# Infini-attention with a parallel silu layer on one core: odd heads' masked score halves, a memory update by pairs of heads, and a new order of the work

## The chip, the cores and the metric

The kernel runs on one core of a Trainium2 chip. The metric is the device time of one execution, in microseconds (us). The kernel before took 229.18 us in the median of three timed runs (228.67 to 229.85). The engines are called by the profile's names: PE is TensorE (PEld its weight loads), ACT ScalarE, DVE VectorE, POOL GpSimd, SP the engine that issues most DMAs.

## The reference, cut to what matters

```python
xn = layernorm(x)                                   # x: 2048 x 512, bf16
# A: 32 heads of 16 dimensions, 4 segments of 512 positions, M and z start at zero
for s in range(4):
    p = softmax(q @ k.T / 4 + causal_mask)          # within the segment
    a_dot = p @ v
    a_mem = (phi(q) @ M) / (phi(q) @ z + 1e-6)      # phi(t) = t + 1 if t > 0 else exp(t)
    o = sigmoid(beta) * a_mem + (1 - sigmoid(beta)) * a_dot
    M = M + phi(k).T @ v;  z = z + phi(k).sum()
A = o @ wo
# B: silu(xn @ w1) @ w2, with w1 512 x 1792
out = x + A + B
```

## The kernel before

**Layout.** Everything that a product contracts lies transposed: 128 features on the partitions, 512 positions of a segment along the row. A tile of 128 features (`dt`, four of them) holds eight heads of 16, so each block of 32 partitions (a group `g`, four of them) holds an even head in its lower and an odd head in its upper 16 rows.

**Scores.** `scores` (L653) makes one *batch*: PE fills a tile `psS` of four PSUM banks (one bank of 512 columns for each `g`), ACT takes the exponential of all 128 x 2048 in one instruction (L669) into a bf16 buffer `Pb`, and POOL zeroes what the causal mask forbids (`affine_select`, L677). The four matmuls of a chunk (one for each `g`) use 32 rows of the array each and run side by side. Keys are taken in blocks of 128 (`kt`), and for a key block only the queries from its first position on are scored: 512, 384, 256 and 128 columns. That is 1280 columns for each parity of head, 2560 for a `dt`, five batches of 512: 80 batches for 4 segments and 4 `dt`. An even head's keys are read from 16 rows of `kT`; an odd head's from all 32 rows of `kTo`, a copy that POOL makes of `kT` with the even rows set to zero (`k_copy`, L359). There is a single `psS`, so the next batch's matmuls wait for the exponential of the last; seven `Pb` buffers hold the weights.

**Weighing.** `weigh` (L687) multiplies the weights by the values: word `E` for the even heads of a `dt`, `O` for the odd ones, each four chunks of 512, 384, 256 and 128 columns, with 32 columns of the array for each `g` (L696). The values carry a block of ones, which gives the softmax's sums. Copies to SBUF and small DMAs bring the sums together (`zraw`), DVE takes reciprocals, DMAs spread them over the rows (`spr<-rz`), and DVE multiplies.

**Memory.** `m_mm` (L415) multiplies phi(k), transposed by DMA, by the values: for each `dt` and each 128 positions one product of 128 x 128, of which `m_mask` (L437) keeps the eight 16 x 16 blocks on the diagonal.

**The other work.** `dense` gives q, k, v and the hidden layer, `out_mm` (L593) the two output products. `product` (L319) issues such a product as one matmul of 128 columns of the array, or, in a stretch that began with a word of kind "cols", as four matmuls of 32 columns that run side by side.

**The order.** The kernel is written under a manual schedule. `ORDER` (L16) is a list of words, each a call of a small function (`S17` the score batch 17, `k0.2.1` a part of the k product of segment 0 and `dt` 2, `kv` its copy on DVE, `ka` on ACT, `h` hidden, `ha` its tanh, `o`, `oc`, `od` output products whole, halved and quartered, `st` an output's store). Each engine runs its instructions in the order of the list, and waits only on semaphores. The list was made by a planner outside the file. Batches carry numbers `20 s + 5 dt + b`; the first is `S1`. The last output tile is stored in two halves (`half_store`, L628) from buffers of their own, `o_half`.

Of the kernel before, what the change touches and what calls it, by code (L numbers as in the profile page):

```python
# [9 lines left out]
ALU = mybir.AluOpType  # L10
BF16 = mybir.dt.bfloat16
# [5 lines left out]
kind odd ones0 ones1 zeros xc0 xd0 xc1 xq0 xi0 Nv0 busy44 xd1 xq1 xc2 xi1 X0.1 Nv1 xd2 Xa0.1 busy6 v0.0.0 v0.0.1 xq2 X1.1 Xa1.1 xs3 v0.0.2 v0.0.3 xq3 v0.1.0 xi2 v0.1.1 v0.1.2 v0.1.3 Nv2 xi3 X2.1 va0.0 k0.2.0 va0.1 Nv3 Xv2.1 X3.1 Xv3.1 k0.0.0 k0.0.1 k0.0.2 k0.0.3 q0.0.0 kv0.0 tb q0.0.1 q0.0.2 xs4 q0.0.3 qa0.0 k0.2.1 q0.3.0 fa0.0 q0.1.0  # L17
S1 k0.2.2 xs6 q0.1.1 v0.3.0 v0.3.1 xs7 q0.3.1 q0.1.2 q0.1.3 xs5 xg4.4 q0.3.2 qa0.1 q0.3.3 fp0.0
S2 k0.2.3 v0.3.2 qv0.3 v0.3.3 k0.1.0 kv0.2 fp0.2 fa0.2 k0.1.1 vv0.3 k0.1.2 k0.1.3 q0.2.0 q0.2.1
S3 kv0.1 q0.2.2 h0.10.0 h0.10.1 Nv4 fv0.0 q0.2.3 h0.10.2 v0.2.0 h0.10.3 qv0.2 ha0.10 k0.3.0 k0.3.1  # L20
S0 Nv5 v0.2.1 k0.3.2 hv0.10 h0.11.0 k0.3.3 h0.11.1 h0.11.2 kv0.3 h0.11.3 Nv7 xs8 XD5 ha0.11 h0.7.0
S7 h0.7.1 h0.1.0 h0.7.2 h0.7.3 v0.2.2 h0.1.1 v0.2.3 XD4 h0.1.2 h0.1.3 hv0.11 Nv6 ha0.7
S6 h0.13.0 fp0.3 XD7 h0.13.1 vv0.2 hv0.7 E0 XD6 v1.1.0 h0.13.2 h0.13.3 ha0.1 v1.1.1 Ev0
S5 fv0.2 h0.5.0 v1.1.2 h0.5.1 hv0.1 v1.1.3 vv1.1 v1.3.0 h0.5.2 ha0.13 xs14 hv0.13 h0.5.3 ha0.5 t0.2 v1.3.1
S9 hv0.5 xs12 q1.1.0 v1.3.2 v1.3.3 fa0.3 q1.1.1 q1.1.2 E1 k1.1.0 q1.1.3
S4 qv1.1 k1.1.1 vv1.3 fv0.3 k1.0.0 k1.0.1 k1.0.2 lw0 h0.4.0 k1.1.2 Ev1 h0.4.1 k1.0.3 k1.1.3 kv1.1
S17 h0.8.0 h0.8.1 kv1.0 h0.4.2 O0 xs10 h0.4.3 h0.2.0 Ov0 ha0.4
S10 h0.2.1 k1.2.0 xs11 xs9 k1.2.1 h0.2.2 k1.2.2 h0.2.3 h0.8.2 ha0.2 t0.3 hv0.4 xg8.4 t0.0 k1.2.3
S8 hv0.2 q1.0.0 q1.0.1 q1.0.2 kv1.2 q1.0.3 h0.8.3 q1.2.0 ha0.8 q1.2.1 q1.2.2 h0.6.0 fp0.1
S13 q1.2.3 h0.6.1 qv1.0 xs15 O1 h0.6.2 qv1.2 Ov1 v1.2.0 Nv11 fa0.1 hv0.8 h0.6.3 Nv9  # L30
S12 h1.11.0 h1.11.1 v1.2.1 fv0.1 h1.11.2 k1.3.0 h1.11.3 k1.3.1 ha0.6 k1.3.2 k1.3.3 Nv10 fp1.1
S11 kv1.3 XD11 v1.2.2 t0.1 v1.2.3 m0.2 ha1.11 hv0.6 q1.3.0 mv0.2 vv1.2 q1.3.1 h0.3.0
S14 fa1.1 h0.0.0 XD9 q1.3.2 q1.3.3 Nv8 h0.3.1 h0.3.2 hv1.11 E2
S15 h0.0.1 h0.0.2 gp1.0 qv1.3 v1.0.0 Ev2 v1.0.1 v1.0.2 xs13 h0.0.3 ha0.0 xg12.4 v1.0.3 fv1.1 h1.9.0 vv1.0 XD8 hv0.0
S16 h1.9.1 h0.3.3 m0.0 h0.9.0 ha0.3 mv0.0 h1.9.2 h1.9.3 ha1.9 XD10 xl0.0 O2
S19 h0.9.1 Ov2 hv1.9 h0.9.2 E3 h0.9.3 h0.12.0 h0.12.1 Nv12 h0.12.2 Ev3 ha0.9
S18 hv0.3 bmask k2.2.0 h1.0.0 h0.12.3 ha0.12 k2.2.1 h1.0.1 h1.0.2 h1.0.3
S22 kv2.2 v2.1.0 hv0.9 hv0.12 ha1.0 tanh O3 h1.8.0 v2.1.1 h1.8.1
S21 h1.8.2 Ov3 v2.2.0 hv1.0 vv2.1 v2.2.1 o0.0.0 o0.0.8 h1.8.3 vv2.2 od0.0.11.1 ha1.8 o0.0.3 Nv14
S23 h1.10.0 hv1.8 o0.0.2 gate sv0 r0.0 xl0.2 oc0.0.13.1 r0.3 o0.0.10 oc0.0.13.0 o0.0.12 k2.1.0 r0.2 h1.4.0 XD14 lw1 o0.0.6  # L40
S20 k2.1.1 kv2.1 h1.4.1 h1.4.2 h1.4.3 r0.1 w0 z0.3 ha1.4 o0.0.5 h1.10.1 h1.10.2 h1.10.3
S24 ha1.10 k2.0.0 k2.0.1 od0.0.11.2 hv1.4 oc0.0.4.0 o0.0.9 kv2.0 E4 od0.0.11.3 od0.0.11.0
S26 fp1.2 o0.2.4 z0.0 o0.2.1 Ev4 fa1.2 o0.2.7 oc0.2.9.0 hv1.10 q2.3.0 zv0.3 o0.2.13 q2.3.1 qv2.3 oc0.2.2.0
S25 h1.5.0 Nv13 h1.5.1 h1.5.2 z0.2 z0.1 o0.0.7 O4 oc0.2.2.1 Ov4 ga1.0 zv0.0 od0.2.0.1
S27 gv1.0 q2.1.0 oc0.2.9.1 o0.0.1 h1.5.3 fv1.2 ha1.5 o0.2.6 q2.1.1 gp1.1 qv2.1 o0.2.17
S29 o0.2.14 o0.2.3 oc0.0.4.1 o0.1.2 zv0.1 zv0.2 fp1.0 o0.1.13 o0.0.14 o0.1.0 ga1.1 hv1.5 oc0.1.12.1 o0.1.6 o0.1.11
S28 o0.2.12 h1.1.0 fa1.0 XD12 h1.1.1 o0.1.14 o0.2.5 o0.0.16 o0.1.16 o0.2.11 mw0.0 h1.1.2
S30 o0.1.9 o0.2.10 mw0.2 od0.2.0.3 h1.1.3 o0.0.17 od0.1.8.1 o0.0.15 o0.2.15 od0.2.0.2 o0.2.8 ha1.1 o0.2.16
S33 fv1.0 st0.0 hv1.1 h1.3.0 od0.2.0.0 h1.3.1 h1.3.2 od0.1.8.3 h1.3.3 Nv15 oc0.1.10.1 XD15 st0.2 XD13 gv1.1 ha1.3 hv1.3 E5 fp1.3 od0.1.8.2 o0.1.4
# [12 lines left out]
S41 r1.0 h2.4.1 ha2.4 vv3.3 v3.0.0 v3.0.1 t2.0 hv2.3 r1.3 w1 h1.7.1 d1.2 h1.7.2 z1.2 h1.7.3
S42 o1.0.0 o1.0.1 vv3.0 d1.3 o1.0.2 v3.1.0 hv2.4 fv2.1 q3.2.0 ha1.7 v3.1.1
S47 q3.2.1 d1.1 oc1.0.4.1 od1.0.5.0 vv3.1 od1.0.5.2 o1.0.12 hv1.7 od1.0.5.1 od1.0.5.3 dv1.2 E8 v3.2.0 qv3.2 d1.0
S44 xl2.1 o1.0.3 h2.8.0 h2.8.1 zv1.2 Ev8 v3.2.1 z1.1 ha2.8 dv1.3 z1.3 oc1.0.9.1 oc1.0.4.0 vv3.2 o1.0.7
S48 gp2.2 k3.2.0 hv2.8 k3.2.1 O8 E9
S49 ga2.3 kv3.2 dv1.1 o1.0.13 k3.0.0 Ev9 Ov8 gv2.2 o1.2.1 k3.0.1 n1.2 kv3.0 o1.2.7 zv1.1 o1.0.11 nv1.2
S51 o1.2.2 h2.0.0 o1.2.8 h2.0.1 gp2.0 o1.0.6 n1.1 ha2.0 o1.2.16
S54 o1.2.11 mw1.0 zv1.3 o1.2.12 od1.2.5.3 nv1.1 z1.0 o1.2.6 o1.0.10 hv2.0 xl2.3 gp2.3 O9 oc1.2.10.1 oc1.0.9.0 Ov9 od1.2.5.2 n1.3 ga2.0
S52 o1.2.4 oc1.2.10.0 oc1.2.0.1 o1.2.15 h2.2.0 dv1.0 h2.2.1 nv1.3 o1.1.3 gv2.0 ha2.2 o1.2.9  # L70
S50 o1.1.0 o1.0.15 oc1.2.0.0 o1.1.17 hv2.2 zv1.0 o1.2.13 n1.0 od1.2.5.0 fp2.2 nv1.0 o1.2.3 fa2.2 od1.1.7.3 o1.0.16 o1.1.15
S53 o1.0.17 od1.2.5.1 oc1.1.9.1 od1.1.7.2 gv2.3 o1.0.8 mw1.2 E10 o1.2.17 o1.2.14 o1.1.11 oc1.1.9.0 ga3.3 Ev10
S55 o1.1.12 st1.2 o1.1.13 h2.7.0 h2.1.0 oc1.1.4.1 fv2.2 h2.7.1 ha2.7 o1.0.14
# [12 lines left out]
S68 d2.0 nv2.3 z2.2 hv3.4 ga3.0 o2.3.12 o2.3.10 o2.3.1 zv2.1 od2.0.7.3 n2.1 o2.0.9 od2.0.7.0 nv2.1 o2.0.12 E13 z2.0
S69 d2.2 O12 Ev13 od2.3.9.1 ga3.2 o2.2.0 od2.3.9.2 dv2.0 oc2.0.2.0 o2.0.15 Ov12 xl2.0 o2.3.17 zv2.2 o2.2.9 od2.2.6.1 n2.0 zv2.0 od2.2.6.3
# [14 lines left out]
def kernel(  # L102
# [731 lines left out]
```

## Time and profile before

| what | us |
|---|---|
| median of three timed runs (lowest, highest) | 229.18 (228.67, 229.85) |
| span of the profiled execution, first to last instruction | 227.4 |
| what the median has beyond that span | 1.8 |
| ACT: 80 exponentials | 150.2 of 198.0 busy |
| ACT: the first and the last exponential start at | 12.72 and 206.62 |
| PE: first matmul starts, last matmul starts | 1.1 and 223.3 |
| POOL: 112 masks | 80.1 of 113.9 busy |
| POOL: 16 copies `kTo` | 11.9 |

The page gives busy times by engine, the span in 40 slices, the chain of work that ended last, and groups of instructions with their count, busy time, mean duration and the idle time before them. Matmuls overlap: one of 512 columns is listed with 380 ns, while the next starts 216 ns later. The granted clock was 1.00 over the span.

### The profile page before, as it was taken

The numbers are of one execution on the slowest core, as the hardware profiler recorded it, in microseconds if no ns is written. First come the engines' busy times: TensorE is split into PE (matmuls) and PEld (weight loads), VectorE is DVE, ScalarE is ACT, GpSimd is POOL, SyncE is SP. The second block draws the span as 40 slices with busy tenths as digits, with TensorE's granted clock in tenths as the row PEclk, the third lists the DMA queues.
The fourth block names the chain that finished last, engine by engine and source line by source line (L and its number), as shares of the span: only waits on it lengthen the run. The fifth ranks groups of instructions, "written<-read, shape, count | busy, mean of one in ns | idle before, by whom it ended". The sixth has DMA issues, their size and how long they took to land.

```text
span 227.4 us, 7543 instructions
## 1 busy us (share of the span) xinstructions
PE 217.2 (96%) x3124; PEld 112.9 (50%) x3152; DVE 177.7 (78%) x351; ACT 198.0 (87%) x179; POOL 113.9 (50%) x173
## 2 busy tenths in 40 slices
PE   8999999999999999999999999999999999999993
PEld 8666645545534434444444434445444444445662
DVE  5799899987787897658798798747676888887834
ACT  3799998999999999999999899999999989897000
POOL 6059647667454673665644577546474265342000
PEclk9999999999999999999999999999999999999999
DMA  6992429323215213404314212141032212024122
GB/s 181 361 381 68 77 52 299 60 55 57 61 22 158 72 35 47 96 15 112 41 40 113 75 53 58 35 117 42 22 100 66 88 36 84 29 63 130 29 90 94
DMA packets 34787, 20.55 MB, mean 90 GB/s; under 512 B 15680, under 2 KB 34240, under 8 KB 34752
## 3 DMA queue, kind: packets, MB, share of 16 engines
q1 hardware_dynamic: 32128, 17.45, 28.3%
q10 hardware_dynamic: 2624, 2.62, 3.6%
q8 instruction: 24, 0.39, 0.8%
q14 instruction: 11, 0.09, 0.1%
HBM read 9.96 MB, written 2.10 MB: 53 GB/s over the span
## 4 chain that ended last, share of the span: by engine, by line
PE 62%; ACT 11%; DVE 11%; DMA 8%; issue 4%; SPq 2%; POOL 0%; DVEq 0%
PE ps L322 18%; PE psO L322 14%; PE psS L662 9%; ACT Pb L669 8%; PE ps L324 8%; PE psO L324 6%; PE psV L696 6%; DMA x_hi<-in_A_x_dram 4%; DMA spr<-rz 3%; ACT th L457 2%; DMA x_res<-in_A_x_dram 2%; DVE stats L272 1%; DVE o_out L586 1%; DVE kT L361 1%; PE psM L324 1%
## 5 line engine op out<-in xcount | busy, mean ns | idle before, releaser
L669 ACT ACTIVATE Pb<-psS 128x2048 bf16<-128x2048 f32 x80 | 150.2, 1878 | 5.8 <-PE psS L662 5.1
L677 POOL TENSOR_SCALAR_AFFINE_SELECT Pb<-Pb 128x512 bf16<-128x512 bf16 (+1 forms) x112 | 80.1, 729 | 85.1 <-ACT Pb L669 83.7
L462 DVE SCALAR_TENSOR_TENSOR hT<-th,ps 128x512 bf16<-128x512 bf16 x56 | 37.8, 679 | 14.1 <-ACT th L457 13.7
L322 PE MATMUL ps<-xnT,w_sb 128*128 128x512 bf16 (+1 forms) x177 | 43.3, 340 | 0.8 <-issue 0.5
L322 PE MATMUL psO<-w_sb,hT 128*128 128x512 bf16 (+2 forms) x139 | 36.1, 340 | 0.7 <-issue 0.5
L457 ACT ACTIVATE th<-ps 128x512 bf16<-128x512 f32 x56 | 32.8, 597 | 0.5 <-PE ps L322 0.4
L324 PE MATMUL psO<-w_sb,hT 128*32 128x128 bf16 (+2 forms) x468 | 26.7, 300 | 0.0
L322 PEld LDWEIGHTS <-w_sb 128*128 128x128 bf16 x184 | 17.1, 98 | 16.3 <-issue 3.3
L696 PE MATMUL psV<-Pb,Vz 128*32 128x128 bf16 (+3 forms) x512 | 23.1, 300 | 0.4 <-DVE oT L573 0.2
L322 PEld LDWEIGHTS <-hT 128*128 128x128 bf16 x149 | 13.6, 97 | 16.9 <-issue 4.8
L324 PE MATMUL ps<-xnT,w_sb 128*32 128x512 bf16 (+1 forms) x384 | 21.8, 329 | 0.0
L324 PEld LDWEIGHTS <-hT 128*32 128x32 bf16 x636 | 15.7, 97 | 9.7 <-issue 1.7
L696 PEld LDWEIGHTS <-Vz 128*32 128x32 bf16 x512 | 13.0, 96 | 10.6 <-issue 1.4
L662 PE MATMUL psS<-qT,kT 16*128 16x128 bf16 (+3 forms) x256 | 17.3, 301 | 0.9 <-ACT Pb L669 0.8
L662 PE MATMUL psS<-qT,kTo 32*128 32x384 bf16 (+3 forms) x256 | 17.2, 299 | 0.6 <-ACT Pb L669 0.2
L362 POOL TENSOR_SCALAR kTo<-kT,pm_odd 128x512 bf16<-128x512 bf16 x16 | 11.9, 747 | 8.2 <-DVE kT L361 7.3
L322 PE MATMUL ps<-xnT,wk_sb 128*128 128x512 bf16 (+1 forms) x66 | 15.4, 328 | 0.7 <-issue 0.5
L322 PE MATMUL ps<-wv_sb,xnT 128*128 128x512 bf16 x48 | 14.3, 380 | 0.6 <-issue 0.2
L662 PEld LDWEIGHTS <-kT 16*128 16x128 bf16 x256 | 5.9, 91 | 16.7 <-issue 16.2
L361 DVE CAST kT<-ps 128x512 bf16<-128x512 f32 x15 | 10.2, 687 | 4.6 <-PE ps L322 4.3
L586 DVE SCALAR_TENSOR_TENSOR o_out<-psO,x_res 128x512 bf16<-128x512 f32 x14 | 9.6, 687 | 5.3 <-PE psO L322 2.8
L719 DVE CAST oraw<-psV 128x512 bf16<-128x512 f32 x16 | 11.0, 688 | 3.4 <-PE psV L696 3.3
(105 smaller groups left out, 298.3 us busy)
## 6 DMA issues: line engine op xcount, KB each, us to landing
spr<-rz SPq DMA_DIRECT2D x56, 64.0 KB
x_res<-in_A_x_dram SPq DMA_DIRECT2D x16, 128.0 KB
out_dram<-o_out SPq DMA_DIRECT2D x15, 128.0 KB
w_sb<-in_B_w_dram SPq DMA_DIRECT2D x1, 1792.0 KB
w_sb<-in_B_w_dram ACTq DMA_DIRECT2D x1, 1792.0 KB
x_hi<-in_A_x_dram SPq DMA_DIRECT2D x2, 512.0 KB
oraw<-odd SPq DMA_DIRECT2D x64, 16.0 KB
wv_sb<-in_A_wv_dram SPq DMA_DIRECT2D x2, 256.0 KB
```

Of the source, the lines that this page charges most:

```text
L322: return [nc.tensor.matmul(out, lhsT=lhsT, rhs=rhs, start=start, stop=stop, skip_group_check=True)]
L324: nc.tensor.matmul(out[c : c + 32], lhsT=lhsT[:, c : c + 32], rhs=rhs, start=start, stop=stop, tile_position=(0, c), skip_group_check=True,)
L361: copy(out=kT[:, dt, :], in_=sts[s].pop(("k", dt))[:, :])
L362: nc.gpsimd.tensor_scalar(out=kTo[:, dt, :], in0=kT[:, dt, :], scalar1=pm_odd[:, 0:1], scalar2=1.0, op0=ALU.mult, op1=ALU.mult,)
L457: nc.scalar.activation(out=th[:], in_=sts[s]["h", ft][:, :], func=AF.Tanh, scale=0.5)
L462: nc.vector.scalar_tensor_tensor(out=st["hT"][:, ft, :], in0=st.pop(("th", ft))[:], scalar=1.0, in1=st.pop(("h", ft))[:, :], op0=ALU.add, ...
L586: out = nc.vector.scalar_tensor_tensor(out=o_out[:], in0=st.pop(("psO", j)), scalar=0.5, in1=st["x", j][:], op0=ALU.mult, op1=ALU.add)
L662: nc.tensor.matmul(psS[:, g, c0 : c0 + nq], lhsT=kk[rows, dt, kt * P : (kt + 1) * P], rhs=st["qT"][rows, dt, kt * P : L], start=True, stop ...
L669: exp = nc.scalar.activation(out=Pb[:, :, :], in_=psS[:, :, :], func=AF.Exp, scale=SCALE)
L677: mask = nc.gpsimd.affine_select(out=blocks, in_=blocks, compare_op=ALU.is_ge, fill=0.0, base=0, pattern=[[0, blocks.shape[1]], [1, P]], c ...
L696: nc.tensor.matmul(psV[32 * g : 32 * g + 32, kt * P : L], lhsT=Vzs[s % 2][:, kt, 4 * dt + g, par : par + 2, :].rearrange("p a d -> p (a d) ...
L719: copy(out=oraw[:], in_=sts[s].pop(("psV", 0))[:, :])
```

## The change

**Scores.** A key block's diagonal square of 128 x 128 has its upper right half of 64 x 64 masked: the second 64 keys against the first 64 queries. Even heads keep their widths (512, 384, 256, 128). For those 64 queries the stationary operand is now `k3[:, kt, 0:P]`: its first 64 columns are the block's first 64 keys with only the even heads' rows kept, its last 64 columns the same 64 keys with only the odd heads' rows kept. So the corner that the mask would empty holds the odd head's scores of the first 64 keys against the first 64 queries; the remaining queries of the chunk are scored from `kT` as before, in a second set of four matmuls. So odd heads' own chunks shrink by 64 columns each (448, 320, 192, 64), and start 64 queries later (from `k3[:, kt, HP:3*HP]`, all 128 keys of the odd head). Two `dt` now share nine batches instead of ten: 72 in all, numbered `18 s + 9 pair + b`.

**Keys.** `k_copy` makes, beside `kT`, a tile `k3` of 192 columns for each key block with two POOL instructions (128 x 512 and 128 x 256) in place of one. Both must be done before any batch of that `dt`; the odd-row mask alone stood behind three of five batches before.

**Masks.** A chunk of an even head is followed by two POOL instructions: one takes the corner out of `Pb` into a tile `low` (64 partitions, 64 columns for each `g`) with its own mask, one masks the square. A chunk of an odd head needs only 64 columns masked. There are 176 mask instructions in place of 112. Seven `low` tiles are set to zero at the start (`lows`).

**Weighing.** `O` adds four chunks of 64 columns that read the `low` tiles: eight chunks of matmuls in place of four.

**Memory.** For each group of 32 rows only that group's two heads' values are multiplied: four matmuls of 32 columns side by side in place of one product of 128 columns; `M32` is a quarter as wide.

**The rest.** Six `Pb` buffers in place of seven; `o_half` takes its buffers from `o_out`'s three; a new list.

```diff
     def k_copy(s, dt, copy=nc.vector.tensor_copy):
-        kT, kTo = seg_tile(s, "kT"), seg_tile(s, "kTo")
+        kT = seg_tile(s, "kT")
+        k3 = sts[s]["k3", dt] = segp.tile([P, TPS, 3 * HP], BF16, name="k3", bufs=6)
         copy(out=kT[:, dt, :], in_=sts[s].pop(("k", dt))[:, :])
-        nc.gpsimd.tensor_scalar(
-            out=kTo[:, dt, :], in0=kT[:, dt, :], scalar1=pm_odd[:, 0:1], scalar2=1.0,
-            op0=ALU.mult, op1=ALU.mult,
-        )
+        k_in = kT[:, dt, :].rearrange("p (t c) -> p t c", c=P)
+        for to, frm, keep in ((k3[:, :, HP : 3 * HP], k_in, pm_odd), (k3[:, :, 0:HP], k_in[:, :, 0:HP], pm_even)):
+            nc.gpsimd.tensor_scalar(
+                out=to, in0=frm, scalar1=keep[:, 0:1], scalar2=1.0, op0=ALU.mult, op1=ALU.mult
+            )
...
     def m_mm(s, d0):
...
-                product(
-                    psM[:, i, :].rearrange("p (h r d) -> p h r d", r=2, d=DH), st["phiK", dt][:, j, :],
-                    Vzs[s % 2][:, j, 4 * dt : 4 * dt + 4, 0:3:2, :], j == 0, j == TPS - 1,
-                )
+                for g in range(4):
+                    nc.tensor.matmul(
+                        psM[32 * g : 32 * g + 32, i, :].rearrange("p (r d) -> p r d", d=DH),
+                        lhsT=st["phiK", dt][:, j, 32 * g : 32 * g + 32],
+                        rhs=Vzs[s % 2][:, j, 4 * dt + g, 0:3:2, :],
+                        start=(j == 0), stop=(j == TPS - 1), tile_position=(0, 32 * g), skip_group_check=True,
+                    )
...
+    def make_lows():
+        for low in lows[0] + lows[1]:
+            nc.gpsimd.memset(low[HP:P], 0.0)
...
-        o_half = work.tile([P, D // 2], BF16, name="o_half", bufs=2)
+        o_half = work.tile([P, D], BF16, name="o_half", tag="o_out", bufs=3)[:, 0 : D // 2]
...
+    ONE = [[(0, 0, 0)], [(0, 0, 3), (0, 0, 1)], [(1, 0, 3), (1, 0, 0)], [(1, 0, 2), (1, 0, 1)]]
+    BATCHES = ONE + [[(0, 0, 2), (0, 1, 2)]] + [[(par, 1, kt) for par, _, kt in chunks] for chunks in ONE]
...
     def scores(t):
...
+            q0 = kt * P + HP
+            parts = [(32, st["k3", dt][:, kt, HP : 3 * HP], c0, q0, L)]
+            if par == 0:
+                parts = [
+                    (32, st["k3", dt][:, kt, 0:P], c0, kt * P, q0),
+                    (16, st["kT"][:, dt, kt * P : (kt + 1) * P], c0 + HP, q0, L),
+                ]
...
+        for first, x in groups:
+            if low is not None:
+                select(low[0:HP, :, x, :].rearrange("p g x c -> p (g x) c"), first[HP:P, :, 0:HP], 0)
+                select(first[:, :, 0:P], first[:, :, 0:P], 0)
+            else:
+                select(first[:, :, 0:HP], first[:, :, 0:HP], HP)
...
-    Pbs = [ppool.tile([P, 4, L], BF16, name=f"Pb{i}") for i in range(7)]
+    Pbs = [ppool.tile([P, 4, L], BF16, name=f"Pb{i}") for i in range(6)]
...
     def weigh(n, par):
...
+        if par == 1:
+            for kt in range(TPS):
+                b, _, _ = PLACE[0, d, kt]
+                x = BATCHES[b].index((0, d, kt))
+                parts.append((kt, st["low", pair, b][:, :, x, :], kt * P, HP))
```

The new list begins, and ends, so:

```text
... k0.0.3 odd kind v0.3.2 v0.3.3 ones0 vv0.0 vv0.3 q0.0.0 q0.0.1 ka0.0 fa0.0 fp0.0 q0.0.2 q0.0.3 qa0.0 q0.2.0 q0.2.1 lows q0.2.2
S1 xs7 k0.1.0 k0.1.1 k0.3.0 k0.1.2 k0.1.3 xs4 fv0.0 k0.3.1 k0.3.2 k0.3.3 xs5 xs6 xg4.4 kv0.1 ka0.3 ones1 fp0.1
S0 q0.1.0 fa0.1 q0.1.1 q0.1.2 q0.2.3 qv0.2 q0.1.3 qv0.1 k0.2.0 k0.2.1
S2 h0.10.0 h0.13.0 h0.10.1 h0.10.2 h0.10.3 ha0.10 Nv6 XD6 Nv7 Nv4 h0.13.1 v0.1.0 h0.13.2 h0.13.3 lw0
S4 ...
... st3.1 o3.0.1 oh10.1 oh14.0 oh2.0 st3.0 oh12.0 oh16.1 oh17.1 sh1 oh7.0 oh15.0 oh10.0 oh9.0 oh13.0 sh0
```

More of the change, by code (lines that the diff above doesn't have):

```diff
@@ L20 @@
[L20 to L25, printed above, removed]
@@ L252 @@
     HL = L // 2
+    HP = P // 2
+    lows = [
+        [cpool.tile([P, 4, n, HP], BF16, name=f"low{n}_{i}") for i in range(bufs)] for n, bufs in ((1, 3), (2, 4))
+    ]
     Zws = [cpool.tile([P, DT, 2, 32], BF16, name=f"Zw{i}") for i in range(2)]
@@ L653, in scores, with wide @@
+    NB = len(BATCHES)
+    def wide(par, kt):
+        return L - kt * P - par * HP
+    PLACE = {}
+    for b, chunks in enumerate(BATCHES):
+        c0 = 0
+        for par, d, kt in chunks:
+            PLACE[par, d, kt] = (b, c0, wide(par, kt))
+            c0 += wide(par, kt)
+        assert c0 == L
+    WEIGHED = [(0, 1, 3, 2), (0, 3, 1, 2)]
     def scores(t):
-        s, dt, b = t // 20, t // 5 % DT, t % 5
+        s, pair, b = t // (2 * NB), t // NB % 2, t % NB
         st = sts[s]
         psS = psatt.tile([P, 4, L], F32, name="psS")
-        for par, kt, c0, nq in BATCHES[b]:
-            for g in range(4):
-                r0 = 32 * g
-                rows = slice(r0, r0 + 16) if par == 0 else slice(r0, r0 + 32)
-                kk = st["kT"] if par == 0 else st["kTo"]
-                nc.tensor.matmul(
-                    psS[:, g, c0 : c0 + nq],
-                    lhsT=kk[rows, dt, kt * P : (kt + 1) * P],
-                    rhs=st["qT"][rows, dt, kt * P : L],
-                    start=True, stop=True, tile_position=(r0, 0),
-                )
@@ L668, in scores @@
-        Pb = st["Pb", dt, b] = Pbs.pop(0)
+        for par, d, kt in BATCHES[b]:
+            dt = 2 * pair + d
+            _, c0, nq = PLACE[par, d, kt]
+            q0 = kt * P + HP
[4 more added lines that the diff above has]
+                    (16, st["kT"][:, dt, kt * P : (kt + 1) * P], c0 + HP, q0, L),
+                ]
+            for n, keys, c, q1, q2 in parts:
+                for g in range(4):
+                    rows = slice(32 * g, 32 * g + n)
+                    nc.tensor.matmul(
+                        psS[:, g, c : c + q2 - q1], lhsT=keys[rows], rhs=st["qT"][rows, dt, q1:q2],
+                        start=True, stop=True, tile_position=(32 * g, 0),
+                    )
```

236 lines of the change are left out of this document (125 added, 111 removed).

## The prediction, as it was put on record

> **What bounds the kernel now.** I read the page's engines and chain first, then the rows of exponentials and masks, then two stretches of the timeline. In section 1 the columns are busy time, share of the span, instructions.
>
> ```profile
> PE 217.2 (96%) x3124; PEld 112.9 (50%) x3152; DVE 177.7 (78%) x351; ACT 198.0 (87%) x179; POOL 113.9 (50%) x173
> ...
> PE 62%; ACT 11%; DVE 11%; DMA 8%; issue 4%; SPq 2%; POOL 0%; DVEq 0%
> ...
> L669 ACT ACTIVATE Pb<-psS 128x2048 bf16<-128x2048 f32 x80 | 150.2, 1878 | 5.8 <-PE psS L662 5.1
> ```
>
> PE is the path for 62% of the span, and ACT is nearly as full. How tightly they are coupled stands in the timeline (start, duration):
>
> ```profile
> 100.54 1.03 PE L322 MATMUL psO<-w_sb,hT 128*128 128x512 bf16 x4
> ...
> 101.50 0.29 PE L662 MATMUL psS<-qT,kT 16*128 16x256 bf16 x4
> ...
> 101.62 0.28 PE L662 MATMUL psS<-qT,kTo 32*128 32x256 bf16 x4
> ...
> 101.83 0.40 PE L324 MATMUL psO<-w_sb,hT 128*32 128x512 bf16 x4
> ...
> 101.95 1.88 ACT L669 ACTIVATE Pb<-psS 128x2048 bf16<-128x2048 f32 x1
> ...
> 102.06 0.61 PE L324 MATMUL ps<-xnT,wq_sb 128*32 128x512 bf16 x8
> ...
> 104.33 1.88 ACT L669 ACTIVATE Pb<-psS 128x2048 bf16<-128x2048 f32 x1
> ```
>
> Four matmuls of 512 columns take 1.03 with 0.38 for the last alone: one every 0.216. Eight of 32 columns do the work of two and take 0.61: the same rate. From the first scores (101.50) to the exponential is 0.45, from there to the next exponential 2.38; 61 of the 79 distances between exponentials are under 2.42. So a batch can't come sooner than about 2.38 after the last: 1.93 until `psS` is free, 0.45 to fill it. Each batch also costs PE two turns between forms of the array: the last whole matmul before it should free PE at 101.40 and scores start at 101.50, the scores end their stream at 101.73 and the next work starts at 101.83. Over all 80 batches the median is 0.10 for each turn.
>
> I then added up PE's work in the order of the list: every matmul by its columns (512 in 0.216), every group of four once, every turn 0.105. From the first scores at 12.25 to the last matmul's start at 223.33 there are 211.1, of which 206.4 are work. Putting the 2.38 rule beside it accounts for 4.4 of waiting on scores, and 0.3 fall to masks. PE bounds the kernel, batches hold it up by 4.4, and POOL by next to nothing.
>
> **The change, part by part** (all against the span of 227.4; the median lies 1.8 above it, and I carry the difference over).
>
> *Scores.* Eight batches fewer: 8 x (0.216 + 2 x 0.105) = -3.4.
>
> *Memory.* 48 products of 128 columns become 48 groups of four matmuls with 32 columns each. A group of 128 columns costs 0.056 by the starts in the trace; the four starts alone take 0.015. No row has 32 columns: bounds are 0.056 (nothing gained) and 0.013 by the stream. I take 0.017, as every group of 128 or more costs its stream plus 0.003: -1.9.
>
> *Small pieces.* 64 even chunks are split in two sets of four, and `O` gets 64 sets more. A second set in a batch costs some 0.012 besides its stream now; a 64-column set is 0.027 of stream. No row shows one set of four row-tiled matmuls following another that is so short: bounds are its stream, 0.027, and 0.109, the shortest such step that there is (256 columns). I take 0.046, near the other end, because the four weight loads of 0.09 start within 0.012 and are not waited for at 101.50: 64 x 0.019 + 0.2 for `O` = +1.4. The high end is +5.1 more, on scores; for `O`, up to 0.056 a set, +1.7.
>
> These three make -3.9, of which 0.3 lies before the first scores, where PE waits anyway: **-3.6**.
>
> *Exponentials and turn-around.* ACT loses 8 x 1.88 = 15, but it was PE that set the end. The new list spaces its batches by 2.48 of PE's work on average, close to the 2.38, so waits remain: the same sum gives 2.4 for 4.4: **-2.0**.
>
> *The start.* The first batch now needs `k3`, so POOL stands between the key copy and S1; before, S1 read `kT` alone. Following the new list with the durations of 3.5 to 12.3: the third tile's turn ends at 10.4 on DVE (one statistic and one copy later than before), the last k part on PE at 10.9, its copy on ACT, behind a table load, at 11.7, POOL's two products at 12.95 (0.70 + 0.44 and the gaps). S1 starts at 13.0 instead of 12.25: **+0.75** (0.3 to 1.3).
>
> *POOL.* Its prices:
>
> ```profile
> L677 POOL TENSOR_SCALAR_AFFINE_SELECT Pb<-Pb 128x512 bf16<-128x512 bf16 x96 | 62.5, 668 | 66.7 <-ACT Pb L669 65.3 <-DVE phiQT L405 1.2
> ...
> L677 POOL TENSOR_SCALAR_AFFINE_SELECT Pb<-Pb 128x1024 bf16<-128x1024 bf16 x16 | 17.6, 1101 | 18.5 <-ACT Pb L669 18.5
> ...
> L362 POOL TENSOR_SCALAR kTo<-kT,pm_odd 128x512 bf16<-128x512 bf16 x16 | 11.9, 747 | 8.2 <-DVE kT L361 7.3
> ...
> L258 POOL MEMSET Zw<- 128x256 bf16 x2 | 0.6, 314 | 0.0
> ```
>
> A line through 512 and 1024 gives 0.45 for 256 elements. A pair of `dt` has six masks of 512, one of 1024, six corners and eight odd masks of 256, and one corner of 512: 12.1, for eight pairs 97 instead of 80. The second key product adds 16 x 0.49 = 8, the `low` tiles 2.7. POOL grows from 114 to 141, 62% of the span: not a bound as a sum, but late at places. And new masks wait for the one before them, since they share tiles. What that costs stands here:
>
> ```profile
> 15.98 0.20 POOL L283 TENSOR_SCALAR rstd_all<-mv_all 128x4 f32<-128x4 f32 x1
> 16.26 1.02 POOL L286 TENSOR_TENSOR rstd_all<-rstd_all,expo 128x4 f32<-128x4 f32 x1
> ```
>
> The second waits for the first: 0.08 of gap; two masks without such a wait overlap by 0.05. So each costs 0.13, and a four-instruction mask 2.35 after its exponential, where a pair took 1.23.
>
> Place by place: after `k3` POOL has `fp0.0`, `lows` (2.7), S1's masks, the roots (1.3), and only then the keys of `dt` 1, done at 21. S4 needs them at 20.2: **+0.75** (0 to 1.5). In before the same queue held one mask pair and no filling. Then the weighings: by this sum the list has `E0`, `O0`, `E1`, `E2`, `E3`, `E7` to `E10` and `E15` arrive 0.2 to 0.8 before their last mask ends: together 3.8 for 0.3: **+3.5** (0.3, if these masks are no slower than the list takes them to be, to 5). With PE waiting there, everything behind it in the list waits.
>
> *Hidden edits.* DVE's memory additions shrink by three quarters: 0.4 each, six of them, beside PE. Six `Pb` cost nothing, since PE's order already puts each weighing before the batch that takes its buffer. The tail has one edit that is not hidden: the list ends `st3.2 st3.1 st3.0 sh1 sh0` on three buffers, and the built order makes both halves wait for an earlier store to land, about 1.3 after its DVE operation by the last stores of the trace. DVE's five operations end some 1.9 after the last matmul starts instead of 1.0; half of it is given back, since SP's last issue stood 0.47 after DVE's end: **+0.5** (0 to 1.2).
>
> Sum: -3.6 - 2.0 + 0.75 + 0.75 + 3.5 + 0.5 = -0.1; **forecast 229.0**, where PE's savings are spent on POOL's delays. Its own range is 227.3 to 230.7.
>
> **Rivals.**
>
> *The list holds (225.3).* If POOL's dependent masks run without the 0.13, the mask waits fall from 3.8 to about 1 and S4's to 0.5, and start and tail are each 0.3 better: -3.7. For it: the new list's weighings then sit right at their masks, as the old one's do (slack of 0.05 to 0.35 in nine places). Against it: the 0.08 gap is there each time that POOL waits for itself.
>
> *Short score sets are held by their loads (233.0, slower).* Place: the 64 split chunks, between the two sets. If the second set's four loads of 128 columns can't be hidden behind 64 columns of stream, the step is the 0.109 of the 256-column row instead of 0.046: 64 x 0.063 = +4.0, on PE and in the turn-around. It decides from 0.065 a set on, where 64 x 0.019 = 1.2 is added. For it: `kT`'s loads take 0.091 each in the page. Against it: transposes on the whole array, with loads of 128 columns too, take 0.39 for four and 0.22 for one, so 0.057 each. The Trainium skill, "TensorE: Matmul & The Clock Gate", section "LDWEIGHTS (loading the stationary operand)", says that a load takes its columns over 1.2 GHz, whatever the rows: 107 ns for 128 columns, an estimate from that page that would give just this rival. The transposes speak against it as a rate, though not for row-tiled loads.
>
> *DVE holds POOL up (231).* Some POOL operations are stretched now:
>
> ```profile
> 19.07 1.02 POOL L362 TENSOR_SCALAR kTo<-kT,pm_odd 128x512 bf16<-128x512 bf16 x1
> ```
>
> It takes 0.70 undisturbed; one mask took 0.94 for 0.64. Where POOL is late, eight such stretches of 0.25 on the way to S4 and the first weighings cost 2.0. For it: DVE is 97% busy from 12 to 25. The Trainium skill, "SBUF — State Buffer", section "SBUF: two separate sides", has these two engines share a pair of ports that one holds for a whole instruction; the stretched rows agree.
>
> That the change doesn't do what it says is excluded: the built order has 72 exponentials.
>
> **Chances.** Forecast 0.46 (within its range, faster by over 0.5% in 0.13, slower in 0.10), list holds 0.21, loads 0.13, DVE 0.14, others 0.06. 0.5% is 1.15, about what a measurement of this kernel can tell. Faster 0.34 (0.13 + 0.21), within 0.5% 0.29 (the forecast's 0.23, DVE's milder 0.04, others 0.02), slower 0.37 (0.10 + 0.13 + 0.10 + 0.04). The range reaches from the list's case to the loads': 225.0 to 233.0.
>
> **What would show it.** First exponential near 13.5; S4 (the fourth) late by over 0.5; PE waiting at weighings for masks; POOL near 141; 72 distances mostly near 2.4 with the last scores near 196; sets of 64 columns at 0.03 to 0.05. Wrong would be: score sets at 0.1, weighings that wait for nothing, or an end set by another engine than PE.

## The result and the profile after

The changed kernel takes 234.57 us in the median of four runs (234.20 to 234.99), the kernel before 228.93 beside it: a ratio of 1.0249, with a 95% interval of 1.0220 to 1.0279. The change makes the kernel 2.5% slower. The forecast was 229.0, and the time lies above its own range (227.3 to 230.7) and above that of all the rivals (225.0 to 233.0). The profiled execution spans 232.5 (227.4 before) and has a mean granted clock of 0.993 (1.000).

From the page of the changed kernel, its engines, its chain, and the rows of the exponentials and masks:

```profile
PE 215.4 (93%) x4012; PEld 117.8 (51%) x4036; DVE 173.7 (75%) x352; ACT 183.8 (79%) x171; POOL 138.6 (60%) x260
...
PE 60%; POOL 13%; ACT 8%; DVE 8%; DMA 5%; issue 4%; POOLq 0%; DVEq 0%
...
L702 ACT ACTIVATE Pb<-psS 128x2048 bf16<-128x2048 f32 x72 | 135.1, 1877 | 16.4 <-PE psS L696 14.9
L716 POOL TENSOR_SCALAR_AFFINE_SELECT Pb<-Pb 128x256 bf16<-128x256 bf16 (+2 forms) x120 | 67.5, 576 | 27.8 <-ACT Pb L702 23.7
L716 POOL TENSOR_SCALAR_AFFINE_SELECT low<-Pb 64x256 bf16<-64x256 bf16 (+1 forms) x56 | 26.7, 477 | 27.9 <-ACT Pb L702 22.0
```

The work is what the prediction made it: 15.1 less of exponentials, masks of 94.2 (97 forecast), POOL at 138.6 (141). The new thing stands in the chain: POOL has 13% of it, where it had 0. DMAs have 5%, less than the 8% before, but 3 of the 5 are the transposes `xnT<-xn_t`, which the page before does not list in its chain. The page's row of idle time says where the exponentials wait: 14.9 for PE's scores, against 5.1.

The chain of the changed kernel in order of time (start, duration) shows the place that costs most:

```profile
13.31 2.67 POOL low L262 x7
...
18.73 1.03 POOL rstd_all L290
...
19.78 0.44 DVE xn_t L305 x2
20.22 7.50 DMA xnT<-xn_t
...
27.77 2.97 PE ps L326 x10
```

This is the layer norm of segment 1: roots on POOL, norms on DVE, transposes by DMA, products on PE. The DMA piece takes 7.5. The timeline of PE, and after it the one of ACT's queue:

```profile
21.21 0.21 PE L696 MATMUL psS<-qT,k 32*128 32x64 bf16 x4 [1.14 <-POOL k L371]
...
27.77 0.41 PE L326 MATMUL ps<-wv_sb,xnT 128*128 128x512 bf16 x1 [3.23 <-DMA xnT<-xn_t]
```

```profile
19.02 0.39 ACTq L168 DMA_DIRECT2D w_sb<-in_B_w_dram  x1
```

At 21.21 S4 has waited for the keys of `dt` 1, as forecast. At 27.77 `v1.2` has waited 3.23 for a transposed tile, which the prediction does not mention. The third line points at a reason: ACT issues the load of `w2`, 1.8 MB, 1.2 before SP issues the first transpose. The new list has the word `lw0` in the line of its third batch, where the old one had it in the line of its ninth (S4):

```diff
-S4 qv1.1 k1.1.1 vv1.3 fv0.3 k1.0.0 k1.0.1 k1.0.2 lw0 h0.4.0 k1.1.2 Ev1 h0.4.1 k1.0.3 k1.1.3 kv1.1
+S2 h0.10.0 h0.13.0 h0.10.1 h0.10.2 h0.10.3 ha0.10 Nv6 XD6 Nv7 Nv4 h0.13.1 v0.1.0 h0.13.2 h0.13.3 lw0
```

The DMA queues of the changed kernel between 20.3 and 25.0 (queue, packets, MB, share of 16 engines; then the issues):

```profile
q10 hardware_dynamic: 1421, 1.46, 93.4%
...
xnT<-xn_t SPq DMA_TRANSPOSE x3
```

q10 is ACT's queue with the load. Three transposes are issued from 20.22 on, and SP's queue, q1, has no packet at all in the stretch; its first one comes at 25.09, 4.9 after the first issue. In the kernel before, the first packet came 1.3 after the issue. The wait also has an aftermath. Stretches of the changed kernel (length; busy time of PE, its loads, DVE, ACT and POOL; then the granted clock):

```profile
27.00:28.00 1.00, 0.23 (x2) 0.12 (x3) 0.00 (x0) 0.00 (x0) 0.93 (x2) 1.00 1.30 197
28.00:29.00 1.00, 1.00 (x6) 0.73 (x5) 0.00 (x0) 0.00 (x0) 0.91 (x3) 0.51 0.17 29
...
30.00:31.00 1.00, 1.00 (x11) 0.18 (x9) 0.23 (x1) 0.00 (x0) 1.00 (x5) 0.50 0.58 52
31.00:32.00 1.00, 1.00 (x32) 0.71 (x32) 1.00 (x2) 0.67 (x1) 0.33 (x1) 0.79 0.06 6
```

From 28.0 to 31.4 PE has half its clock: 3.4 of work at half speed, 1.7 lost on top of the wait.

To see all of it I followed PE's matmuls from the first scores to the last, with their streams and 0.10 for each turn; what is left over at a place is waiting there. The stretch grew from 211.1 to 215.8, while its work shrank by some 3.7.

| PE waits (us) | before | after |
|---|---|---|
| for transposes, and the half clock behind it | 0 | 3.4 + 1.7 |
| S4 for keys | 0 | 1.3 |
| scores for the last exponential | 2.1 | 1.3 |
| weighings (`E`, `O`) for masks or for a bank | 1.1 | 4.5 |
| the rest | 1.5 | 0.9 |

So two theories. **Loads:** the load of `w2` keeps the transposes from moving. **POOL's queue** (what the prediction's reasons would say): `lows` and S1's four masks stand ahead of the roots, which come at 18.45 instead of 15.98; norms and transposes are late by that, and the load does nothing.

### The profile page after: what moved, and what is told of

It reads as the page before. It is cut to its first block, busy times and chain, and to the rows that moved or that the text cites. A ratio compares the mean times of both kernels' runs of the same rounds, so it can differ in the third digit from the quotient of the medians.

```text
span 232.5 us, 9449 instructions
## 1 busy us (share of the span) xinstructions
PE 215.4 (93%) x4012; PEld 117.8 (51%) x4036; DVE 173.7 (75%) x352; ACT 183.8 (79%) x171; POOL 138.6 (60%) x260
## 4 chain that ended last, share of the span: by engine, by line
PE 60%; POOL 13%; ACT 8%; DVE 8%; DMA 5%; issue 4%; POOLq 0%; DVEq 0%
PE ps L326 16%; PE psO L328 13%; PE ps L328 8%; PE psS L696 7%; PE psO L326 7%; ACT Pb L702 6%; PE psV L754 6%; POOL Pb L716 5%; DMA xnT<-xn_t 3%; POOL low L716 3%; PE psS L328 3%; POOL k L371 2%; DMA x_lo<-in_A_x_dram 1%; POOL low L262 1%; DVE stats L276 1%
## 5 line engine op out<-in xcount | busy, mean ns | idle before, releaser
L702 ACT ACTIVATE Pb<-psS 128x2048 bf16<-128x2048 f32 x72 | 135.1, 1877 | 16.4 <-PE psS L696 14.9
L716 POOL TENSOR_SCALAR_AFFINE_SELECT Pb<-Pb 128x256 bf16<-128x256 bf16 (+2 forms) x120 | 67.5, 576 | 27.8 <-ACT Pb L702 23.7
L716 POOL TENSOR_SCALAR_AFFINE_SELECT low<-Pb 64x256 bf16<-64x256 bf16 (+1 forms) x56 | 26.7, 477 | 27.9 <-ACT Pb L702 22.0
L328 PE MATMUL psO<-w_sb,hT 128*32 128x512 bf16 (+2 forms) x668 | 42.2, 328 | 0.0
L472 ACT ACTIVATE th<-ps 128x512 bf16<-128x512 f32 x56 | 33.1, 594 | 5.9 <-PE ps L328 5.3
L326 PE MATMUL ps<-xnT,w_sb 128*128 128x256 bf16 (+1 forms) x169 | 35.6, 332 | 0.3 <-issue 0.2
L328 PE MATMUL ps<-xnT,w_sb 128*32 128x512 bf16 (+1 forms) x432 | 26.9, 353 | 0.0
L696 PE MATMUL psS<-qT,k 32*128 32x64 bf16 (+3 forms) x512 | 23.3, 235 | 2.1 <-POOL k L371 1.1
L754 PE MATMUL psV<-Pb,Vz 128*32 128x320 bf16 (+7 forms) x512 | 22.5, 287 | 2.8 <-POOL Pb L716 1.6
L326 PE MATMUL psO<-w_sb,hT 128*128 128x512 bf16 (+2 forms) x91 | 21.4, 312 | 1.1 <-issue 1.0
L696 PE MATMUL psS<-qT,kT 16*128 16x448 bf16 (+3 forms) x256 | 14.9, 269 | 0.0
L328 PE MATMUL psO<-wo_sb,oT 128*32 128x512 bf16 x152 | 14.4, 380 | 0.0
```

The lines of the kernel that those rows point to most:

```text
L326: return [nc.tensor.matmul(out, lhsT=lhsT, rhs=rhs, start=start, stop=stop, skip_group_check=True)]
L328: nc.tensor.matmul(out[c : c + 32], lhsT=lhsT[:, c : c + 32], rhs=rhs, start=start, stop=stop, tile_position=(0, c), skip_group_check=True,)
L472: nc.scalar.activation(out=th[:], in_=sts[s]["h", ft][:, :], func=AF.Tanh, scale=0.5)
L696: nc.tensor.matmul(psS[:, g, c : c + q2 - q1], lhsT=keys[rows], rhs=st["qT"][rows, dt, q1:q2], start=True, stop=True, tile_position=(32 * ...
L702: exp = nc.scalar.activation(out=Pb[:, :, :], in_=psS[:, :, :], func=AF.Exp, scale=SCALE)
L716: over[id(Pb)].append(nc.gpsimd.affine_select(out=out, in_=in_, compare_op=ALU.is_ge, fill=0.0, base=base, pattern=[[0, out.shape[1]], [1, ...
```

## The experiments

Each list edit is shown as the words around it. "Before" is the kernel before on the same chip, 228.5 to 229.0 in these sets.

**e1_w2_later**

In the lines of S2 and S8:

```diff
-h0.13.3 lw0
+h0.13.3
...
-v1.3.3 lw1 h0.2.0
+v1.3.3 lw0 lw1 h0.2.0
```

> The changed kernel with one word of its list moved: the load of w2 (1.8 MB, issued by ACT at 19.0 us, ahead of S4) goes to the place of the load of wo, some 15 us later. Theory B (the load is what holds up the layer norm's transposes: they are issued from 20.2 on, but no 256-byte packet of theirs moves before 25.0, when the load is nearly through): the wait of 3.2 before v1.2 goes, and with it the 3.4 us at half clock behind it (1.7 of work): 234.6 - 4.9 = 229.7, and a mean granted clock of 1.000 for 0.993. Theory A (POOL's queue is late with the roots, so norms and transposes are late): nothing changes, 234.6.

Measured 236.17, slower still; yet the wait at `v1.2` is gone, with the roots as late as ever (the first transpose is issued at 20.25). What came instead, in ACT's timeline and PE's:

```profile
32.32 0.39 ACTq L168 DMA_DIRECT2D w_sb<-in_B_w_dram  x1
...
38.10 0.39 ACTq L168 DMA_DIRECT2D wo_sb<-in_A_wo_dram  x1
```

```profile
40.95 0.62 PE L696 MATMUL psS<-qT,k 32*128 32x192 bf16 x8 [4.00 <-ACT Pb L702]
```

The second load on ACT's queue is issued only 5.8 after the first; by the profile's releaser it had waited for a small move of the sums to `zraw` to land. That move, issued by SP at 32.72, has its first packet only at 37.30: the load of `w2` holds it up as it held the transposes. The tanh and the exponential behind it in ACT's order stood still for 4.3. The loads theory is right about the transposes; its time fails because the edit made a wait of the same size elsewhere, with twice the stretch at half clock (6.8, mean clock 0.985).

**e2_lows_first** and **e3_both**

```diff
-q0.2.1 lows q0.2.2
+q0.2.1 q0.2.2
...
-xc0 xd0 xq0
+lows xc0 xd0 xq0
```

> The changed kernel with the word lows moved to the front of the list, where POOL is idle: the seven memsets (2.67) no longer stand ahead of S1's masks, the roots and the keys of dt 1. Theory A: the roots come 1.1 earlier (masks from 15.0 on instead of 16.06), S4's wait of 1.1 goes, norms and transposes are 1.1 earlier, and if they land 1.1 earlier too, 233.4; if the wait before v1.2 then falls short of halving the clock, 231.7. Theory B: the transposes still move only when the load of w2 is through, at 25 to 27.8; what S4 gains is waited for at v1.2: 234.6.

Measured 234.84. S4's wait fell from 1.14 to 0.16, and `v1.2` waited 3.54 instead. The transposes, issued 0.85 earlier, were held up as before (first packet at 24.12, 4.75 after the issue), and `v1.2` started 0.54 earlier, at 27.23 for 27.77. So the loads theory is right that the wait stays; that the transposes move only when the load is through is not so, since it ended at 27.4. Of POOL's lateness at the roots at most 0.54 counts here, and the time shows nothing of it. In three of the four executions the mean clock was 0.985 and the time 234.8; the fourth kept 0.999 and took 232.3. So 2.5 lie between executions with the half clock and without.

> Both moves together. Theory B with A's part for S4: -4.9 for w2 and -1.1 for S4's wait: 228.6, about the kernel before. By the rival that the rest of the list is what costs (mask waits, short score sets), one of the two moves would already give all, and this one no more than it: 229.7. If the change's savings of PE work (3.6 by the prediction, 3.2 with the memory groups at the 0.025 that the trace shows) come through undiminished: 226 or below.

Measured 234.80. It has e1's stall at the load of `wo` (4.18), so it decides nothing about the rest; the next experiments avoid that stall.

**e4_pairs_alone**: the kernel before with the changed kernel's `m_mm`, the narrower `M32` and its `m_mask`.

> The kernel before with the memory update by pairs of heads alone, its own list kept. 48 products of 128 columns at 0.056 become groups of four at 0.025 (the step that the changed kernel's trace shows, where the prediction took 0.017): -1.5, 227.4. If PE's savings there are eaten by waits of the list: 228.9. With the prediction's size: -1.9, 227.0.

Measured 229.00 beside 228.49 (ratio 1.0034, 1.0001 to 1.0067): nothing gained. The page's waits of PE say where part of it went: on the last exponential 1.6 instead of 0.9. In the profiled execution the stretch from the first scores to the last matmul is 0.7 shorter (210.4 for 211.0), half of the 1.5 that was forecast: what PE saves between two batches it waits away in part, and the rest doesn't show in the times, which spread from 227.7 to 230.3.

**e5_w2_wo_later**: as e1, but `lw1` goes on to S19, `fv1.0 lw1 h1.9.2`.

> The changed kernel with the load of w2 moved to the place of the load of wo, as in e1_w2_later, and the load of wo moved on by some 30 us, to S19, so that ACT never issues a load while the one before it is under way. In e1_w2_later ACT stood for 4.3 at the issue of wo (38.10), 5.4 after that of w2, and PE for 4.0 behind it, at half clock afterwards. Theory B (the transposes wait for w2's load): no wait at v1.2, none at wo, clock 1.000: 234.6 - 3.2 - 1.7 = 229.7. Theory that the list loses its time wherever it is relieved (the end is set by something else): 234 to 236 again.

Measured 232.74, clock 0.998. Between 20.3 and 25.0 SP's queue now moves its packets:

```profile
q1 hardware_dynamic: 1625, 0.39, 41.9%
```

The wait and the half clock, 5.1, are gone, but only 1.8 of the time. Two things took the rest. The weighings wait 6.1 instead of 4.5: while PE stood still in the changed kernel, POOL had caught up with its masks (`E0` and `O0`, which did not wait there, wait 0.8 and 0.65 here). And the load of `wo` made a new wait; e6 shows both of its ends, DVE at the small moves of the sums, PE behind it.

**e6_and_lows**: e5 with `lows` in front.

> e5_w2_wo_later with lows at the front of the list too. Theory: S4's wait (1.1, of which 0.2 stayed in e2_lows_first) is no longer hidden by the wait for the transposes, so 0.9 is gained on e5: 228.8. If S4's wait lies beside another one later on: 229.7.

Measured 231.93: 0.8 gained on e5, near the 0.9 forecast. With the load out of the way, POOL's early queue does cost what the prediction put on S4. The timelines of DVE and of PE:

```profile
67.92 0.35 DVE L501 TENSOR_SCALAR zsum<-zraw,evec 128x256 f32<-128x256 bf16 x1 [1.38 <-DMA zraw<-odd]
```

```profile
72.26 0.59 PE L326 MATMUL ps<-xnT,w_sb 128*128 128x512 bf16 x2 [1.32 <-DVE qT L379]
```

**e7_w2_early_in_before**: the reverse, in the kernel before.

```diff
-h0.11.3 Nv7
+h0.11.3 lw0 Nv7
...
-k1.0.2 lw0 h0.4.0
+k1.0.2 h0.4.0
```

> The kernel before with one word moved: the load of w2 from 32.5 us to about 19, ahead of the layer norm's transposes. Theory B: the transposes' packets, which start at 22.0 there, now start only when the load is nearly through, 5.4 after its issue, at 24.5 or later; the first product that reads tile 5 (25.9) and those of tile 7 (28) wait 1.5 to 4, with some microseconds of half clock if it comes to more than 3: 230 to 234. Theory A (the load does the transposes nothing, POOL's queue is what was late): 228.5.

Measured 234.08 beside 228.50 (ratio 1.0245, 1.0173 to 1.0318). One moved word costs the old kernel as much as the whole change does:

```profile
29.78 0.62 PE L324 MATMUL ps<-wv_sb,xnT 128*32 128x512 bf16 x4 [3.71 <-DMA xnT<-xn_t]
```

with half clock from 29.7 to 33.1 behind it. The first transpose was issued as early as ever, at 20.97 (20.94). POOL's queue as the reason for the transposes has fallen.

**e8_wo_between**: e6 with `lw1` at S22, `r0.2 w0 lw1 h0.6.3`.

> e6_and_lows with the load of wo moved from S19 to S22, behind the last reciprocal (r0.2) of segment 0. In e6_and_lows that load (0.5 MB, issued at 63.65) lay ahead of the small moves of the weighing's sums to zraw; DVE's zsum at 67.92 waited 1.38 for one of them, and PE 1.49 at 72.26 behind the copies that DVE was late with. Theory (any bulk load holds up the small transfers issued after it): that wait goes, 231.9 - 1.5 = 230.4. If the place does not matter: 231.9.

Measured 230.05 beside 228.94 (1.0054, 1.0038 to 1.0070). The wait of 1.5 is gone. This is the change with its loads and its memsets put where they meet nothing: still 1.1 slower than before. From first scores to last matmul it takes 211.0, as the kernel before did; 5.9 of it are waits at weighings. The 1.1 lie at the ends: S1 starts 0.5 later (12.74), and 4.8 instead of 4.1 pass after the last matmul's start.

**e9_lows_of_both_first**

```diff
-        for first, x in groups:
-            if low is not None:
-                select(low[0:HP, :, x, :].rearrange("p g x c -> p (g x) c"), first[HP:P, :, 0:HP], 0)
+        if low is not None:
+            for first, x in groups:
+                select(low[0:HP, :, x, :].rearrange("p g x c -> p (g x) c"), first[HP:P, :, 0:HP], 0)
+        for first, x in groups:
+            if low is not None:
                 select(first[:, :, 0:P], first[:, :, 0:P], 0)
```

> e8_wo_between with the masks of a batch of two even chunks in another order: both corner masks first, then both diagonal ones, so that one instruction of the four waits for POOL itself instead of three. By the prediction's 0.13 for each such wait, these sets (16 of 72 batches) end 0.26 earlier. If that is what makes the weighings late: up to 1.5 is gained of the 4.2 that PE stands waiting for masks in e6_and_lows, 229. If POOL is late because of all that is queued, and not because of its own waits: within 0.5 of e8_wo_between, about 230.2.

Measured 228.43, 1.6 less than e8: waits at weighings 4.3 for 5.9. By the traces a set of four masks takes 2.07 in the median for 2.30, 0.12 less for each of the two waits taken away. So part of what POOL waits for itself is paid by PE.

**e10_weighings_later**: e8 with eight words moved, for instance

```diff
-ha0.11 E0 h0.7.0 h0.7.1 h0.7.2
+ha0.11 h0.7.0 h0.7.1 h0.7.2 E0
```

> e8_wo_between with eight weighings (E0, O0, E2, E3, E7, E8, E9, E10) each moved behind one to three pieces of other PE work (0.2 to 0.65 us) that the list has right after it. In e6_and_lows PE stands 4.7 in all at these eight. Theory (the list puts them ahead of their masks, and PE could do other work meanwhile): -3.4, 227.0, about 1.5 below the kernel before. Rival (the waiting only moves on to the next scores or the next bank, since exponentials come every 2.38 at best): 229.5 to 230.4.

Measured 232.01, slower by 2.0 than e8. By the page, waits of `psV` for masks fell from 2.0 to 0.3; but the copies behind the moved weighings free their banks later, and later products and sums wait (0.53 at 28.80, 0.86 at 53.88, 1.49 at 72.67, 0.74 at 94.76, all for DVE). The rival holds, and more: the weighing stands early because others wait for what it frees.

**e11_no_corners**

```diff
-            nc.gpsimd.memset(low[HP:P], 0.0)
+            nc.gpsimd.memset(low[:], 1.0)
...
-                select(low[0:HP, :, x, :].rearrange("p g x c -> p (g x) c"), first[HP:P, :, 0:HP], 0)
```

> e8_wo_between without the 56 masks that copy the odd heads' corners out of the even heads' blocks; the odd heads are weighed with constants there instead, so this part of the result is left out. POOL falls by 27, from 139 to 112 as in the kernel before, and every mask set by 0.5 to 1. Theory (the 4.2 of waiting for masks is POOL's lateness and on the path): 230.4 - 3.7 = 226.7. Rival (banks and DVE end the same waits): 229 or more.

Measured 225.48 beside 228.94 (0.9871, 0.9819 to 0.9923): 4.6 less than e8. The waits at weighings fall to 1.1, those of the kernel before. (Its profile is of the slowest of its four executions, with half clock at the start and the first scores 2.6 late; counted from there, 206.2 to the last matmul.) So 4.6 is the price of the corners' masks in time.

**e12_own_halves** and what followed

```diff
-        o_half = work.tile([P, D], BF16, name="o_half", tag="o_out", bufs=3)[:, 0 : D // 2]
+        o_half = work.tile([P, L], BF16, name="o_half", tag="odd")[:, 0 : D // 2]
```

> e9_lows_of_both_first with the last tile's two halves in buffers that have been free for long (those of the odd heads' copies) instead of the three of o_out. In e9's trace DVE waits 1.28 for the store of an o_out to land before it computes the first half (223.29), and the span ends 4.4 after the last matmul's start, against 4.05 in the kernel before. Theory (this wait is on the path): -0.4 to -1.0, 227.4 to 228.0 where e9 has 228.4. Rival (SP's three stores ahead in its queue and their landing set the end): within 0.2 of e9.

Measured 227.47 beside 228.98: ratio 0.9939, 0.9912 to 0.9966. DVE's last operations in e9, then in e12:

```profile
223.29 0.76 DVE L648 SCALAR_TENSOR_TENSOR o_half<-psS,x_res 128x256 bf16<-128x256 f32 x2 [1.28 <-DMA out_dram<-o_out]
```

```profile
221.99 0.97 DVE L648 SCALAR_TENSOR_TENSOR o_half<-psS,x_res 128x256 bf16<-128x256 f32 x2
```

The wait is gone and 1.0 is gained. With this, the changed kernel with its loads, memsets, masks and last buffers put in order beats both kernels, the one before by 0.6%.

**e14_pool_later**, three pieces of POOL's work moved out of the way of masks:

> e12_own_halves with three pieces of POOL's work taken out of the way of masks: zeros (0.56) and ones1 (0.95) go to the front of the list beside lows, and gp2.0 (0.61) behind E10. In e9's trace PE waits 0.64 for masks at O0, right behind zeros, 0.68 at E10, right behind gp2.0. Theory (POOL's queue ahead of the masks is what remains): -1.0 to -1.3 on e12, about 226.5, below the kernel before by 1%. Rival (PE then waits at the next scores instead): within 0.4 of e12.

Measured 228.57, 1.1 more than e12. Waits for masks fell (2.7 to 1.4), but the start came late: POOL's memsets and the norm on DVE, in e14's timelines, and the same norm in e12:

```profile
5.27 1.85 POOL L848 MEMSET Vz<- 128x1024 bf16 x2
```

```profile
5.26 2.00 DVE L305 TENSOR_SCALAR xn_t<-x_lo,mv_all,rstd_all 128x512 bf16<-128x512 bf16 x1
```

```profile
5.35 0.53 DVE L305 TENSOR_SCALAR xn_t<-x_lo,mv_all,rstd_all 128x512 bf16<-128x512 bf16 x1
```

DVE's instruction was held until POOL's two memsets were through. PE then waited 1.34 at the first turn and, in the profiled execution, ran at half clock from 9.4 to 12.8; by the mean clock six of the twelve executions did so. The others took 228.0 to 228.5, still more than e12.

**e15_two_pool_later**, the same without the two moves to the front:

> e12_own_halves with zeros moved from S4 to S13, where POOL is idle for 1.5, and gp2.0 behind E10; ones1 stays, and nothing goes to the front of the list. Theory: the waits for masks at O0 (0.64) and E10 (0.68) go or shrink as in e14_pool_later (2.72 to 1.40 in all), and the start stays as in e12_own_halves: 227.5 - 1.0 = 226.5, about 1% below the kernel before. Rival (e14_pool_later's gain of 0.7 between first scores and last matmul was the later start's own): 227.3 or more.

Measured 227.65 beside 228.46 (0.9961, 0.9944 to 0.9978), the same as e12 within the spread. The waits at `O0` and `E10` shrank by 0.5 and 0.4, and those at `E3` and `E9` grew by 0.5 and 0.25: the waiting moved on. What POOL has queued ahead of single masks is not the limit; the sum of masks is (e11).

## Why the prediction was wrong, step by step

**The step that failed** is the sum "place by place" over POOL's queue and the absence of any term for the list's DMAs. It names the roots ("S1's masks, the roots (1.3), and only then the keys of `dt` 1"), follows the keys to S4, and leaves the roots there; it never goes on to the norms, the transposes and the products that wait for them, and it never looks at `lw0`, which the new list moves ahead of the transposes. That place cost 3.4 of waiting and 1.7 of half clock (e5 against the changed kernel, e7 in reverse). In e7 the time grew by 5.6, as the wait and the half clock say; in the changed kernel moving the load gave back 1.8 at first (e5), because other waits took its place. The roots' lateness, which the step did see, makes no wait at `v1.2` by itself (e1: late roots, no wait); with the load ahead it is worth 0.5 there at most (e2).

**PE's work, -3.6:** right (-3.7), by some luck, since two sizes are off against each other. A group of four 32-column matmuls takes 0.025 (0.017 forecast), +0.4; a 64-column set takes 0.038 in the median (0.046), -0.5. S1's four sets in PE's timeline, the first three 0.03 to 0.04 apart:

```profile
12.62 0.21 PE L696 MATMUL psS<-qT,k 32*128 32x64 bf16 x4
12.65 0.20 PE L696 MATMUL psS<-qT,kT 16*128 16x64 bf16 x4
12.69 0.20 PE L696 MATMUL psS<-qT,k 32*128 32x64 bf16 x4
12.72 0.30 PE L696 MATMUL psS<-qT,kT 16*128 16x320 bf16 x4
```

That ends the rival of the loads of short sets (233.0): the time is near it, and for another reason. What the forecast took for granted is that such savings arrive in the time. Those of the memory update alone did not (e4).

**Waits on scores, -2.0:** too large, -0.8 (2.1 to 1.3). Of the 4.4 that the 2.38 rule seemed to explain in the kernel before, half were waits for banks and copies. **The start, +0.75:** +0.35, S1 at 12.62. **S4, +0.75:** a wait of 1.3, of which 0.8 is gained when `lows` goes (e6 against e5).

**Weighings, +3.5:** right in the changed kernel (1.1 to 4.5), but by luck: there the stall let POOL catch up with its masks. Once the load is out of the way the term is too small (6.1). All ten weighings that the prediction names wait in e6, and one more, `E5`. The 0.13 for POOL's wait for itself is borne out (0.12, e9): two of the three such waits in each set of four masks taken away gain 1.6 in time. So the rival "the list holds" is refuted; it would have needed e11's waits.

**The tail, +0.5:** the sharing costs 1.0 (e12 against e9); in the changed kernel DVE has the same wait, of 0.91, and yet the span ends 4.1 after the last matmul's start, as before; what is shorter at its end was not tried.

**DVE holds POOL up (231):** seen in part. Two pairs of masks of the changed kernel, and DVE's operation beside the first:

```profile
62.82 1.23 POOL L716 TENSOR_SCALAR_AFFINE_SELECT Pb<-Pb 128x256 bf16<-128x256 bf16 x2
...
65.96 0.78 POOL L716 TENSOR_SCALAR_AFFINE_SELECT Pb<-Pb 128x256 bf16<-128x256 bf16 x2 [0.74 <-ACT Pb L702]
```

```profile
62.86 0.92 DVE L413 SCALAR_TENSOR_TENSOR pk<-ex,pos 128x512 bf16<-128x512 bf16 x1
```

The first pair takes 0.45 more than the second, and the same DVE operation takes 0.69 at 13.64. From that pair on POOL has no pause up to the last mask of `E3`, for which PE waits 0.7. So some of the waits at weighings are such stretches; no run takes them apart from the masks themselves. e14 shows the reverse, POOL holding DVE, for 1.5.

Without the load's place the forecast would have been nearer, though not right. With loads and memsets moved, e8 takes 230.05, inside the forecast's own range of 227.3 to 230.7; but the memsets' place was part of the forecast, and by e6 it costs 0.8. An estimate for the loads alone is thus 230.9, 0.2 above the range. No run has just that.

## What to carry to other kernels

When a list of work is new, follow every DMA that it moves, bulk loads above all, and ask which small transfer is issued while they run: one moved word was worth as much as the whole change. Follow each late producer to the last engine that waits for its result, and price a wait of PE of 1.8 or more with the half clock that can follow it. A saving on the busiest engine is only worth what the next wait leaves of it: here 3.7 of PE's work was gone, and POOL's small dependent instructions took 4.6 back.

## What the runs showed of the hardware

**A bulk load on one queue holds up what is issued on the other.** With the load of `w2` on ACT's queue, SP's transposes have their first packet 4.9 after the first issue in the changed kernel, 4.75 in e2 and 4.3 in e7, when 1.5, 1.1 and 1.2 MB of the load have passed; without it 1.3 after (e5 and the kernel before). From then on both queues move together: in the changed kernel the load's last packet is at 26.9. The 0.5 MB of `wo` does the same to plain small moves: in e6 one issued at 63.71 has its first packet 2.9 later, in e8, without the load there, 1.1 later. What ends the hold isn't shown. The Trainium skill, "DMA: Bandwidth & Descriptors", section "Queues, rings and completion order", says that each DMA engine goes round the queues that have work, packet by packet. By that rule the transposes would have been slowed from their start and not stopped; the measurement differs, and decides.

**Half clock after a window in which PE idles for over half.** The stretches at 0.50 ahead of the last matmul are 3.41 long (the changed kernel, e7, e11, e14) or 6.83 (e1, e2, e3), and never anything between. I cut the 16 traces into windows of 3.41 that start where the clock changes, and added up the time in each without a matmul of PE. In the seven windows ahead of a halving it is 1.76 to 3.41 (3.17 in the changed kernel); in no window at full clock that another one followed is it more than 1.33. A half window with 0.9 or more was followed by another, one with at most 0.4 by full clock; so e2's wait of 3.54, spread over two windows, led to 6.83. The Trainium skill, "TensorE: Matmul & The Clock Gate", section "Part 1: The HAM clock gate (the "warmup" mystery)", has the clock halved after an idle window of about 3.4 and restored after as much steady work, with windows that run freely. The traces agree with the length and with free windows. They differ on the idle window: 1.8 of idling in one sufficed, and the measurement decides. The execution of e2 that escaped has no trace, so that its wait fell otherwise on the windows is not shown.
